# An attention and dense kernel with a hand-written order: third buffer for the input, seven norms on GpSimd, constants first, last stores on two queues, another order

## The chip, the cores and the metric

One Trainium2 chip, one core of it. The metric is device time in microseconds (us) of one execution. Five engines run side by side, each through its own instructions in order: TensorE (PE; its weight loads are PEld), VectorE (DVE), ScalarE (ACT), GpSimd (POOL) and SyncE (SP), which here only issues DMAs. They wait for each other by semaphores.

## What is computed

x is 2048 rows of 512. It is normalised row by row; the result xn feeds two branches, and both are added to x.

```python
x = A_x
xn = _layernorm(x, axis=-1)
return x + _A_ref(xn, A_wq, A_wk, A_wv, A_wo, A_beta) + _B_ref(xn, B_w1, B_w2)
# _B_ref: silu(xn @ w1) @ w2, with 1792 hidden columns
# _A_ref: 32 heads of 16, 4 segments of L = 512 rows; for each segment s:
logits = jnp.einsum('bhqd,bhkd->bhqk', qs, ks) * scale + mask
a_dot = jnp.einsum('bhqk,bhkd->bhqd', _softmax(logits), vs)
num = jnp.einsum('bhld,bhde->bhle', phi(qs), M)
den = jnp.einsum('bhld,bhd->bhl', phi(qs), z)[..., None] + 1e-06
o = g * num / den + (1.0 - g) * a_dot        # then o @ wo over all segments
M, z = M + phi(ks)^T vs, z + sum(phi(ks))    # phi(t): t + 1 above 0, exp(t) below
```

## The kernel before

**Order.** Nothing is scheduled by the framework. The string ORDER (lines 16 to 98) holds words, and the loop at the end of the kernel (from line 795) calls for each word a small function that emits its instructions. So the place of a word in the list is the place of its instructions in the queue of every engine that it uses, its DMAs on SP's included. Each line of the list begins with an S word. There are 80; the stretch from one to the next is called a section here.

**Words.** `S`t (scores, line 653): t counts segment, group dt of 8 heads (four) and batch b (five); four row-tiled matmuls per part write the 4-bank PSUM tile psS, of which there is one; the exponential of 2048 columns on ScalarE (L669) makes Pb, and GpSimd masks its diagonal blocks (L677), one pass or two. `E` and `O` (weigh, L696) multiply Pb with v into a PSUM bank psV for the even and odd heads; `Ev`, `Ov` copy it out on DVE and `Ea`, `Oa` on ScalarE (L719, L726), and each then issues DMAs on SP: two that gather sums into zraw (L711) and, for odd heads, four that move rows into oraw (L730). `k`, `q`, `v`, `h` are the dense products, in parts of half or a quarter; `kv`, `qv`, `vv` copy their banks on DVE, `va`, `qa`, `ka` on ScalarE; `kv` also makes kTo on GpSimd (L362), the masked copy that half of the scores read. `ha`, `hv` are tanh on ScalarE and the rest of silu on DVE (L457, L462). `fp`, `fa`, `fv` make phi(K) on GpSimd, ScalarE and DVE, `gp`, `ga`, `gv` phi(Q) in the tile phiQT; `t`, `m`, `mv`, `mw` the memory M. `s`, `sv`, `r`, `w` and `R`, `W` are the denominators and their reciprocals (R and W for the last segment); `z`, `d` spread them by two DMAs each on SP (L542), `zv`, `dv` multiply by them, `n`, `nv` the memory's product and its addition to oT. `o`, `oc`, `od`, `oh` are parts of the output products over 14 rows of hT (0 to 13) and 4 of oT (14 to 17); `st` and `sh` add x and store.

**Norms.** `xs` (or `xc`, `xd`) takes the statistics of a tile of 128 rows, `xg` the roots for four tiles on GpSimd (L283, L286), `Nv`t the norm on DVE and `Na`t the same on GpSimd (ln_norm, L301). Tiles 0 to 3 are turned by TensorE (`X`), the others by a transposing DMA on SP (`XD`, L749).

**Buffers.** x tiles 0 to 3 lie in x_lo, which takes oT's buffer, 4 to 11 in x_hi, one of two hT buffers, 12 to 15 in x_end, one of two phiQT buffers. PSUM has eight banks: four for psS, four that all other products share, each free again when its copy has run. In the last segment psS becomes the place of the outputs of row tiles 2 and 3 once the last exponential has read it.

**Shapes.** Score matmuls use row tiles of the array, E and O column tiles; the dense products behind an S word are emitted whole (L322) or in four column tiles (L324) so as to fit the next such word.

Of the kernel before, what the change touches and what calls it, by code (L numbers as in the profile page):

```python
# [25 lines left out]
S4 qv1.1 k1.1.1 vv1.3 fv0.3 k1.0.0 k1.0.1 k1.0.2 lw0 h0.4.0 k1.1.2 Ev1 h0.4.1 k1.0.3 k1.1.3 kv1.1
S17 h0.8.0 h0.8.1 kv1.0 h0.4.2 O0 xs10 h0.4.3 h0.2.0 Ov0 ha0.4
S10 h0.2.1 k1.2.0 xs11 xs9 k1.2.1 h0.2.2 k1.2.2 h0.2.3 h0.8.2 ha0.2 t0.3 hv0.4 xg8.4 t0.0 k1.2.3
S8 hv0.2 q1.0.0 q1.0.1 q1.0.2 kv1.2 q1.0.3 h0.8.3 q1.2.0 ha0.8 q1.2.1 q1.2.2 h0.6.0 fp0.1
S13 q1.2.3 h0.6.1 qv1.0 xs15 O1 h0.6.2 qv1.2 Ov1 v1.2.0 Nv11 fa0.1 hv0.8 h0.6.3 Nv9  # L30
S12 h1.11.0 h1.11.1 v1.2.1 fv0.1 h1.11.2 k1.3.0 h1.11.3 k1.3.1 ha0.6 k1.3.2 k1.3.3 Nv10 fp1.1
S11 kv1.3 XD11 v1.2.2 t0.1 v1.2.3 m0.2 ha1.11 hv0.6 q1.3.0 mv0.2 vv1.2 q1.3.1 h0.3.0
S14 fa1.1 h0.0.0 XD9 q1.3.2 q1.3.3 Nv8 h0.3.1 h0.3.2 hv1.11 E2
S15 h0.0.1 h0.0.2 gp1.0 qv1.3 v1.0.0 Ev2 v1.0.1 v1.0.2 xs13 h0.0.3 ha0.0 xg12.4 v1.0.3 fv1.1 h1.9.0 vv1.0 XD8 hv0.0
S16 h1.9.1 h0.3.3 m0.0 h0.9.0 ha0.3 mv0.0 h1.9.2 h1.9.3 ha1.9 XD10 xl0.0 O2
S19 h0.9.1 Ov2 hv1.9 h0.9.2 E3 h0.9.3 h0.12.0 h0.12.1 Nv12 h0.12.2 Ev3 ha0.9
S18 hv0.3 bmask k2.2.0 h1.0.0 h0.12.3 ha0.12 k2.2.1 h1.0.1 h1.0.2 h1.0.3
S22 kv2.2 v2.1.0 hv0.9 hv0.12 kind ha1.0 tanh O3 h1.8.0 v2.1.1 h1.8.1
# [5 lines left out]
S25 h1.5.0 Nv13 h1.5.1 h1.5.2 z0.2 z0.1 o0.0.7 O4 oc0.2.2.1 Ov4 ga1.0 zv0.0 od0.2.0.1
S27 gv1.0 q2.1.0 oc0.2.9.1 o0.0.1 h1.5.3 fv1.2 ha1.5 o0.2.6 q2.1.1 gp1.1 qv2.1 o0.2.17
S29 o0.2.14 o0.2.3 oc0.0.4.1 o0.1.2 zv0.1 zv0.2 fp1.0 o0.1.13 o0.0.14 o0.1.0 ga1.1 hv1.5 oc0.1.12.1 o0.1.6 o0.1.11
S28 o0.2.12 h1.1.0 fa1.0 XD12 h1.1.1 o0.1.14 o0.2.5 o0.0.16 o0.1.16 o0.2.11 mw0.0 h1.1.2
S30 o0.1.9 o0.2.10 mw0.2 od0.2.0.3 h1.1.3 o0.0.17 od0.1.8.1 o0.0.15 o0.2.15 od0.2.0.2 o0.2.8 ha1.1 o0.2.16
S33 fv1.0 st0.0 hv1.1 h1.3.0 od0.2.0.0 h1.3.1 h1.3.2 od0.1.8.3 h1.3.3 Nv15 oc0.1.10.1 XD15 st0.2 XD13 gv1.1 ha1.3 hv1.3 E5 fp1.3 od0.1.8.2 o0.1.4
# [7 lines left out]
S39 od0.3.10.0 oc0.3.11.1 h1.2.0 o0.3.8 o0.3.16 kv3.1 gv1.3 h1.2.1 h1.2.2 oc0.3.11.0 xl1.2 E7 fa2.3
S43 gv1.2 h1.2.3 od0.3.10.2 ha1.2 o0.3.7 qv3.3 o0.3.1 O7 od0.3.10.1 fp2.3 Ev7 Ov7 m1.2 oc0.3.13.1
S45 o0.3.12 q3.0.0 hv1.2 ga2.2 q3.0.1 q3.1.0 q3.1.1
S40 mv1.2 m1.0 o0.3.17 oc0.3.13.0 qv3.0 fp2.1 qv3.1 fv2.3 mv1.0 fa2.1 o0.3.15 s1 o0.3.3 st0.3 sv1 h2.3.0  # L60
S46 r1.2 r1.1 h2.3.1 h2.4.0 v3.3.0 ha2.3 xl1.0 v3.3.1 h1.7.0
S41 r1.0 h2.4.1 ha2.4 vv3.3 v3.0.0 v3.0.1 t2.0 hv2.3 r1.3 w1 h1.7.1 d1.2 h1.7.2 z1.2 h1.7.3
# [11 lines left out]
S57 t2.1 o1.1.2 o1.1.14 st1.0 o1.1.6 h2.1.1 o1.1.8 t2.3 hv2.7 h2.11.0 oc1.1.4.0 ha2.1 od1.1.7.1 od1.1.7.0
S56 h2.11.1 o1.1.5 ha2.11 o1.3.0 o1.3.16 o1.3.15 gp2.1 o1.3.14 o1.3.8 xl1.1 hv2.1 o1.1.10 xl1.3
S59 o1.1.1 o1.1.16 O10 hv2.11 oc1.3.10.1 o1.3.3 o1.3.4 ga2.1 h2.6.0 st1.1
S58 Ov10 gp3.3 E11 oc1.3.1.0 gv2.1 m2.0 o1.3.13 Ev11 h2.6.1 ha2.6 o1.3.11 mv2.0
S62 h2.5.0 O11 h2.5.1 o1.3.5 hv2.6 od1.3.12.0 od1.3.12.3 Ov11 ha2.5 s2 hv2.5 gv3.3
S60 od1.3.12.1 h2.13.0 h2.13.1 od1.3.12.2 o1.3.9 ha2.13 o1.3.2 hv2.13 o1.3.7 o1.3.6 oc1.3.1.1
S64 k3.3.0 gp3.0 o1.3.17 oc1.3.10.0 st1.3 k3.3.1 h2.10.0 h2.10.1 ka3.3 ha2.10 sv2  # L80
S61 o2.3.0 h3.1.0 r2.2 h2.9.0 o2.3.5 h2.9.1 oc2.3.2.1 oc2.3.13.1 h3.1.1 r2.0 r2.1 r2.3 o2.3.3 xl3.2 ha2.9 hv2.10 gp3.2 ha3.1
S63 o2.3.6 o2.3.4 t2.2 o2.3.11 w2 hv3.1 h3.3.0 h3.3.1 hv2.9 ha3.3 m2.2
S67 d2.1 d2.3 mv2.2 fill z2.3 hv3.3 h3.0.0 oc2.3.2.0 E12 h3.0.1 ha3.0 Ev12 h3.4.0
S66 hv3.0 od2.3.9.3 o2.0.3 dv2.1 o2.0.0 h3.4.1 h2.12.0 h2.12.1 ha2.12 o2.0.10 zv2.3 hv2.12
S65 o2.0.4 oc2.3.13.0 o2.0.13 o2.0.11 oc2.0.6.1 dv2.3 o2.0.5 o2.3.8 o2.3.7 n2.3 z2.1 o2.0.1 mw2.2 ha3.4
# [748 lines left out]
```

## Time and profile before

| what | value |
|---|---|
| three runs, median (lowest to highest) | 229.09 us (228.93 to 229.31) |
| the profiled execution, its own time | 229.25 us |
| its span, first to last instruction | 227.4 us |
| granted TensorE clock | 1.000 |
| first scores, 80th scores (L662) | 12.45, 205.48 us |
| exponentials (L669) | 80, mean 1878 ns, 150.2 us together |
| masks (L677) | 112, mean 720 ns |
| norms on DVE (L301): x_lo, x_hi, x_end | 413, 535, 499 ns mean |
| idle of ScalarE before exponentials for want of scores | 4.0 us in 9 waits |

In the profile a line gives start and length in us, engine, line of the kernel, operation, tiles written and read, shapes and count; square brackets hold idle time before it and what ended it. SPq and ACTq are issues of DMAs. A busy TensorE is not one at its peak, since matmuls are pipelined and their ends are modelled; the distance of two starts tells what one takes.

### The profile page before, as it was taken

Reading aid. Unit: us, or ns where it says so; the run is one execution under the profiler, and the core shown is the slowest. Engines: PE = TensorE matmul, PEld = TensorE weight load, DVE = VectorE, ACT = ScalarE, POOL = GpSimd, SP = SyncE. Lnnn points to the kernel's source line nnn. Section 1 sums busy time; section 2 is a strip of 40 time slices with the busy share of each in tenths; the row PEclk is TensorE's granted clock in tenths of the full one; section 3 lists DMA queues with packets and bytes.
Section 4 is the critical chain, followed back from the end, with each engine's and each line's share of the span. In section 5 each row is a group of like instructions: output and inputs, shape, how many; then the busy total and the mean of one; then the engine's idle time right before and its main releaser. Section 6 shows DMA issues by size and latency. Waiting matters only on the chain.

```text
span 227.4 us, 7551 instructions
## 1 busy us (share of the span) xinstructions
PE 217.5 (96%) x3127; PEld 113.3 (50%) x3155; DVE 177.1 (78%) x350; ACT 198.5 (87%) x180; POOL 113.9 (50%) x173
## 2 busy tenths in 40 slices
PE   8999999999999999999999999999999999999993
...
ACT  3799998999999999999999899999999989897000
...
GB/s 189 369 379 46 85 36 313 62 45 66 61 22 156 73 35 48 95 34 100 36 61 87 90 45 59 32 119 40 37 93 65 80 40 81 31 68 128 16 95 95
DMA packets 34787, 20.55 MB, mean 90 GB/s; under 512 B 15680, under 2 KB 34240, under 8 KB 34752
## 3 DMA queue, kind: packets, MB, share of 16 engines
...
q8 instruction: 24, 0.39, 0.7%
...
HBM read 9.96 MB, written 2.10 MB: 53 GB/s over the span
## 4 chain that ended last, share of the span: by engine, by line
PE 67%; ACT 17%; DVE 7%; issue 4%; POOL 2%; DMA 1%; DVEq 0%; SPq 0%; ACTq 0%
PE ps L322 20%; PE psO L322 13%; ACT Pb L669 12%; PE psO L324 8%; PE psS L662 8%; PE ps L324 6%; PE psV L696 5%; PE psS L324 3%; ACT th L457 3%; PE psS L756 2%; ACT ex L395 1%; DVE hT L462 1%; DVE kT L361 1%; DVE qT L371 1%; DVE xn_t L301 1%
## 5 line engine op out<-in xcount | busy, mean ns | idle before, releaser
L669 ACT ACTIVATE Pb<-psS 128x2048 bf16<-128x2048 f32 x80 | 150.2, 1878 | 4.7 <-PE psS L662 4.0
L677 POOL TENSOR_SCALAR_AFFINE_SELECT Pb<-Pb 128x512 bf16<-128x512 bf16 (+1 forms) x112 | 79.1, 720 | 84.3 <-ACT Pb L669 83.0
L462 DVE SCALAR_TENSOR_TENSOR hT<-th,ps 128x512 bf16<-128x512 bf16 x56 | 37.7, 679 | 14.4 <-ACT th L457 13.7
L322 PE MATMUL ps<-xnT,w_sb 128*128 128x512 bf16 (+1 forms) x177 | 43.3, 340 | 0.8 <-issue 0.5
L322 PE MATMUL psO<-w_sb,hT 128*128 128x512 bf16 (+2 forms) x137 | 36.0, 339 | 0.7 <-issue 0.5
L457 ACT ACTIVATE th<-ps 128x512 bf16<-128x512 f32 x56 | 32.8, 598 | 0.6 <-PE ps L322 0.6
L324 PE MATMUL psO<-w_sb,hT 128*32 128x512 bf16 (+2 forms) x476 | 27.6, 301 | 0.0
L322 PEld LDWEIGHTS <-w_sb 128*128 128x128 bf16 x184 | 17.1, 98 | 16.3 <-issue 3.3
L696 PE MATMUL psV<-Pb,Vz 128*32 128x128 bf16 (+3 forms) x512 | 23.1, 300 | 0.2
L324 PE MATMUL ps<-xnT,w_sb 128*32 128x512 bf16 (+1 forms) x384 | 21.8, 329 | 0.0
L322 PEld LDWEIGHTS <-hT 128*128 128x128 bf16 x147 | 13.4, 98 | 16.6 <-issue 4.8
L324 PEld LDWEIGHTS <-hT 128*32 128x32 bf16 x644 | 15.9, 97 | 9.3 <-issue 1.7
L662 PE MATMUL psS<-qT,kT 16*128 16x128 bf16 (+3 forms) x256 | 17.3, 301 | 0.9 <-ACT Pb L669 0.8
L696 PEld LDWEIGHTS <-Vz 128*32 128x32 bf16 x512 | 13.1, 96 | 10.3 <-DVE hT L462 1.1
L662 PE MATMUL psS<-qT,kTo 32*128 32x384 bf16 (+3 forms) x256 | 17.2, 299 | 0.6 <-ACT Pb L669 0.2
L362 POOL TENSOR_SCALAR kTo<-kT,pm_odd 128x512 bf16<-128x512 bf16 x16 | 12.3, 771 | 8.4 <-DVE kT L361 7.5
L322 PE MATMUL ps<-xnT,wk_sb 128*128 128x512 bf16 (+1 forms) x66 | 15.4, 328 | 0.7 <-issue 0.5
L322 PE MATMUL ps<-wv_sb,xnT 128*128 128x512 bf16 x48 | 14.3, 380 | 0.6 <-DVE odd L726 0.2
L662 PEld LDWEIGHTS <-kT 16*128 16x128 bf16 x256 | 5.9, 91 | 16.7 <-issue 16.2
L361 DVE CAST kT<-ps 128x512 bf16<-128x512 f32 x15 | 10.2, 689 | 4.9 <-PE ps L322 4.3
L322 PE MATMUL ps<-xnT,wq_sb 128*128 128x256 bf16 (+1 forms) x62 | 12.8, 324 | 0.4 <-issue 0.2
L726 DVE CAST odd<-psV 128x512 bf16<-128x512 f32 x15 | 10.3, 687 | 3.5 <-PE psV L696 3.4
...
## 6 DMA issues: line engine op xcount, KB each, us to landing
...
oraw<-odd SPq DMA_DIRECT2D x64, 16.0 KB
...
```

Of the source, the lines that this page charges most:

```text
L322: return [nc.tensor.matmul(out, lhsT=lhsT, rhs=rhs, start=start, stop=stop, skip_group_check=True)]
L324: nc.tensor.matmul(out[c : c + 32], lhsT=lhsT[:, c : c + 32], rhs=rhs, start=start, stop=stop, tile_position=(0, c), skip_group_check=True,)
L361: copy(out=kT[:, dt, :], in_=sts[s].pop(("k", dt))[:, :])
L362: nc.gpsimd.tensor_scalar(out=kTo[:, dt, :], in0=kT[:, dt, :], scalar1=pm_odd[:, 0:1], scalar2=1.0, op0=ALU.mult, op1=ALU.mult,)
L457: nc.scalar.activation(out=th[:], in_=sts[s]["h", ft][:, :], func=AF.Tanh, scale=0.5)
L462: nc.vector.scalar_tensor_tensor(out=st["hT"][:, ft, :], in0=st.pop(("th", ft))[:], scalar=1.0, in1=st.pop(("h", ft))[:, :], op0=ALU.add, ...
L662: nc.tensor.matmul(psS[:, g, c0 : c0 + nq], lhsT=kk[rows, dt, kt * P : (kt + 1) * P], rhs=st["qT"][rows, dt, kt * P : L], start=True, stop ...
L669: exp = nc.scalar.activation(out=Pb[:, :, :], in_=psS[:, :, :], func=AF.Exp, scale=SCALE)
L677: mask = nc.gpsimd.affine_select(out=blocks, in_=blocks, compare_op=ALU.is_ge, fill=0.0, base=0, pattern=[[0, blocks.shape[1]], [1, P]], c ...
L696: nc.tensor.matmul(psV[32 * g : 32 * g + 32, kt * P : L], lhsT=Vzs[s % 2][:, kt, 4 * dt + g, par : par + 2, :].rearrange("p a d -> p (a d) ...
L726: copy(out=odd[:], in_=sts[s].pop(("psV", 1))[:, :])
L756: nc.tensor.matmul(idle[:, 0:P], lhsT=zraw[:, 0:P], rhs=zraw[:, 0:P], start=True, stop=True)
```

## The change

A third home for x: tiles 8 to 11 go to x_mid, the first use of the tag phiQT, and x_end is the second. x_hi now holds tiles 4 to 7 alone. Norms 4, 6, 8, 9, 10, 12 and 14 are `Na` words. `kind` and `odd` (DVE) stand at the head of the list. v0.3 is copied by ScalarE (`va0.3`) and q0.1 by DVE (`qv0.1`). The stores of the last segment's even row tiles and of the first half of its last one go to ScalarE's queue. And the whole list has another order; the number of matmul columns is the same.

```diff
+    x_mid = segp.tile([P, TPS, D], BF16, name="x_mid", tag="phiQT")
     x_end = segp.tile([P, TPS, D], BF16, name="x_end", tag="phiQT")
 
     def xs(t0, t1):
         if t0 >= NT - TPS:
             return x_end[:, t0 - NT + TPS : t1 - NT + TPS, :]
+        if t0 >= 2 * TPS:
+            return x_mid[:, t0 - 2 * TPS : t1 - 2 * TPS, :]
         return x_lo[:, t0:t1, :] if t1 <= TPS else x_hi[:, t0 - TPS : t1 - TPS, :]
...
     def store(s, j):
...
-        nc.sync.dma_start(out=out_flat[t * P : (t + 1) * P, :], in_=o_out[:])
+        queue = nc.scalar if s == LAST and j % 2 == 0 else nc.sync
+        queue.dma_start(out=out_flat[t * P : (t + 1) * P, :], in_=o_out[:])
...
     def half_store(h):
...
-        nc.sync.dma_start(out=out_flat[(NT - 1) * P : NT * P, cols], in_=o_half[:])
+        queue = nc.sync if h else nc.scalar
+        queue.dma_start(out=out_flat[(NT - 1) * P : NT * P, cols], in_=o_half[:])
```

The list, its head and its end (the middle is left out):

```diff
 ORDER = """
-ones0 ones1 zeros xc0 xd0 xc1 xq0 xi0 Nv0 busy44 xd1 xq1 xc2 xi1 X0.1 Nv1 xd2 Xa0.1 busy6 v0.0.0 v0.0.1 xq2 X1.1 Xa1.1 xs3 v0.0.2 v0.0.3 xq3 v0.1.0 xi2 v0.1.1 v0.1.2 v0.1.3 odd Nv2 xi3 X2.1 va0.0 k0.2.0 va0.1 Nv3 Xv2.1 X3.1 Xv3.1 k0.0.0 k0.0.1 k0.0.2 k0.0.3 q0.0.0 kv0.0 tb q0.0.1 q0.0.2 xs4 q0.0.3 qa0.0 k0.2.1 q0.3.0 fa0.0 q0.1.0
-S1 k0.2.2 xs6 q0.1.1 v0.3.0 v0.3.1 xs7 q0.3.1 q0.1.2 q0.1.3 xs5 xg4.4 q0.3.2 qa0.1 q0.3.3 fp0.0
-S2 k0.2.3 v0.3.2 qv0.3 v0.3.3 k0.1.0 kv0.2 fp0.2 fa0.2 k0.1.1 vv0.3 k0.1.2 k0.1.3 q0.2.0 q0.2.1
-S3 kv0.1 q0.2.2 h0.10.0 h0.10.1 Nv4 fv0.0 q0.2.3 h0.10.2 v0.2.0 h0.10.3 qv0.2 ha0.10 k0.3.0 k0.3.1
-S0 Nv5 v0.2.1 k0.3.2 hv0.10 h0.11.0 k0.3.3 h0.11.1 h0.11.2 kv0.3 h0.11.3 Nv7 xs8 XD5 ha0.11 h0.7.0
-S7 h0.7.1 h0.1.0 h0.7.2 h0.7.3 v0.2.2 h0.1.1 v0.2.3 XD4 h0.1.2 h0.1.3 hv0.11 Nv6 ha0.7
-S6 h0.13.0 fp0.3 XD7 h0.13.1 vv0.2 hv0.7 E0 XD6 v1.1.0 h0.13.2 h0.13.3 ha0.1 v1.1.1 Ev0
-S5 fv0.2 h0.5.0 v1.1.2 h0.5.1 hv0.1 v1.1.3 vv1.1 v1.3.0 h0.5.2 ha0.13 xs14 hv0.13 h0.5.3 ha0.5 t0.2 v1.3.1
...
-S74 o2.3.16 h3.12.0 st2.3 h3.12.1 ha3.12 h3.2.0 gv3.1 E14
-S73 h3.2.1 ha3.2 Ev14 oc2.2.5.1 o2.1.2 o2.2.16 o2.1.6 hv3.12 h3.8.0 o2.2.10 st2.2 hv3.2 o2.1.1 o2.1.5 h3.8.1 ha3.8 hv3.8
-S79 o2.1.0 O14 Ov14 od2.1.12.2 s3 sv3 r3.1 o2.1.7 r3.3 h3.7.0 r3.2 r3.0 oc2.1.10.0 od2.1.12.3 o2.1.3 w3
-S77 h3.6.0 R0.0 oc2.1.11.0 h3.7.1 R0.1 ha3.7 h3.6.1 hv3.7 d3.2 o2.1.14 R0.3 h3.9.0 ha3.6 hv3.6 o2.1.15
-S76 o2.1.8 d3.0 d3.1 h3.9.1 o2.1.9 oc2.1.10.1 h3.13.0 ha3.9 od2.1.12.0 oc2.1.11.1 h3.13.1 xl3.3 hv3.9 o3.0.12 o2.1.16 ha3.13 o2.1.13
-S75 o3.0.5 hv3.13 o2.1.4 o3.0.4 R0.2 W0 o2.1.17 z3.0 h3.10.0 o3.1.8 h3.10.1 dv3.0 z3.2 ha3.10 od2.1.12.1 st2.1 o3.0.0 o3.1.6
-S78 o3.0.9 hv3.10 dv3.1 o3.1.1 h3.11.0 o3.0.8 h3.11.1 dv3.2 E15 oh13.1 oh4.1 ha3.11 z3.1 o3.2.13 Ea15 oh12.1 hv3.11 oh6.1 oh10.1 o3.2.1 O15 Oa15 oh11.1 oh2.1 oh12.0 o3.0.1 zv3.0 oh13.0 n3.1 od3.1.11.3 oh3.1 zv3.1 o3.2.0 oh10.0 n3.0 o3.1.2 nv3.0 o3.0.7 nv3.1 o3.1.12 oh9.1 oh8.0 o3.2.5 oh11.0 o3.1.7 o3.2.6 o3.0.13 oh8.1 R1.1 R1.0 o3.2.9 o3.1.14 d3.3 R1.3 o3.2.14 oc3.0.3.0 oh0.0 o3.0.6 o3.2.8 oc3.0.11.1 zv3.2 o3.1.10 n3.2 o3.2.10 oh9.0 R1.2 oh1.1 oh15.0 W1 nv3.2 oh15.1 o3.2.4 oc3.0.11.0 o3.1.5 o3.0.14 o3.2.11 oh1.0 o3.2.12 o3.2.2 oh6.0 o3.2.16 oh2.0 z3.3 oh7.0 oh0.1 dv3.3 oh3.0 od3.0.10.0 oh14.0 od3.1.11.1 oc3.1.0.0 o3.0.15 zv3.3 od3.1.11.0 oc3.0.3.1 n3.3 oc3.1.9.0 oh4.0 o3.2.3 xl3.0 o3.1.16 nv3.3 o3.2.15 od3.0.10.1 od3.0.10.2 o3.2.7 oh5.0 oh16.0 oh16.1 od3.0.10.3 oh14.1 o3.2.17 oh17.0 oh17.1 o3.0.2 o3.0.16 o3.0.17 od3.1.11.2 xl3.1 st3.2 oc3.1.9.1 oh7.1 oh5.1 sh0 o3.1.17 sh1 oc3.1.0.1 o3.1.3 o3.1.15 o3.1.13 st3.0 o3.1.4 st3.1
+kind odd ones0 ones1 zeros xc0 xd0 xc1 xq0 xi0 Nv0 busy44 xd1 xq1 xc2 xi1 X0.1 Nv1 xd2 Xa0.1 busy6 v0.0.0 v0.0.1 xq2 X1.1 Xa1.1 xs3 v0.0.2 v0.0.3 xq3 v0.1.0 v0.1.1 va0.0 xi2 Nv2 v0.1.2 v0.1.3 tb X2.1 xi3 Nv3 k0.2.0 X3.1 k0.2.1 Xv2.1 k0.0.0 k0.0.1 Xv3.1 k0.0.2 k0.0.3 q0.0.0 va0.1 kv0.0 q0.0.1 q0.0.2 q0.0.3 k0.2.2 k0.2.3 qa0.0 v0.3.0 fa0.0
+S0 xs4 q0.3.0 q0.3.1 k0.1.0 v0.3.1 v0.3.2 v0.3.3 kv0.2 va0.3 xs6 xs5 fp0.2 q0.3.2 q0.1.0 k0.1.1
+S2 q0.3.3 k0.3.0 qv0.3 k0.1.2 xs7 q0.1.1 k0.3.1 q0.1.2 xg4.4 q0.1.3 fa0.2 qv0.1 Na4 k0.3.2 k0.1.3
+S1 h0.1.0 kv0.1 k0.3.3 h0.10.0 h0.10.1 q0.2.0 h0.1.1 h0.10.2 kv0.3 h0.10.3 ha0.10
+S5 h0.7.0 fv0.2 Nv5 h0.7.1 tanh t0.2 h0.7.2 Na6 q0.2.1 h0.7.3 h0.1.2 q0.2.2 h0.1.3 ha0.7 hv0.10 q0.2.3 xs8 xs10
+S6 v0.2.0 v0.2.1 qv0.2 v0.2.2 Nv7 h0.11.0 h0.11.1 h0.11.2 v0.2.3 h0.11.3 hv0.7 vv0.2 ha0.1 XD5
+S3 v1.1.0 h0.5.0 v1.1.1 h0.5.1 XD4 hv0.1 h0.5.2 XD7 v1.1.2 ha0.11 v1.1.3 h0.5.3 vv1.1 h0.13.0 ha0.5 XD6 fp0.1 hv0.5
+S7 h0.13.1 xs9 h0.13.2 E0 h0.13.3 ha0.13 v1.3.0 hv0.11 v1.3.1
+S4 Ev0 v1.3.2 fp0.3 v1.3.3 hv0.13 E1 k1.2.0 xs11 k1.2.1 fa0.3 q1.1.0 Ev1 q1.1.1 xg8.4 vv1.3
...
+S25 h1.3.0 o0.2.14 gv1.0 h1.3.1 h1.3.2 h1.1.2 o0.2.15 h1.1.3 oc0.1.12.1 o0.2.16 ha1.1 Nv13 XD13 od0.2.0.1 od0.1.8.0 fp1.2
...
+S60 h2.9.0 h3.1.0 h3.1.1 hv2.10 o2.3.5 h2.9.1 h3.3.0 xl2.3 o2.3.1 ha3.1 r2.0 w2 hv3.1 d2.1 ha2.9 hv2.9
...
+S73 oc2.1.10.1 h3.2.1 xl3.2 hv3.12 o2.1.3 xl3.1 hv3.5 h3.8.0 xl3.3 gv3.0 E14 oc2.1.10.0 ha3.2 Ev14 hv3.2 h3.8.1 ha3.8 hv3.8
+S77 od2.1.12.3 o2.1.2 O14 h3.6.0 Ov14 s3 sv3 h3.6.1 o2.1.13 ha3.6
+S78 r3.0 od2.1.12.1 r3.1 h3.13.0 h3.9.0 oc2.1.11.0 r3.2 h3.9.1 ha3.9 hv3.6 r3.3 h3.13.1 o2.1.5 w3 ha3.13
+S76 d3.2 h3.10.0 od2.1.12.0 hv3.13 o2.1.16 R0.0 h3.10.1 R0.1 ha3.10 hv3.9 hv3.10 o2.1.1 o2.1.9 R0.3 o2.1.15 o3.0.4 R0.2 W0 o3.0.5 dv3.2
+S75 d3.1 o2.1.14 h3.7.0 h3.7.1 h3.11.0 o2.1.4 d3.0 ha3.7 o3.0.0 o3.0.6 hv3.7 o3.0.9 h3.11.1 o3.0.13 ha3.11
+S79 o2.1.8 o3.1.7 oc3.0.3.1 o2.1.17 hv3.11 o3.1.1 o3.0.8 z3.2 E15 oc3.0.11.0 od2.1.12.2 o3.1.8 dv3.1 zv3.2 z3.0 oh4.1 od3.1.11.2 z3.1 o3.1.6 o3.2.3 oh1.0 oc3.1.9.0 o3.1.5 st2.1 dv3.0 zv3.1 O15 Ea15 od3.0.10.3 od3.1.11.0 zv3.0 oh3.0 o3.2.5 oh9.0 o3.1.12 n3.1 o3.2.12 Oa15 oh5.1 oh11.1 oc3.0.3.0 oh11.0 o3.2.11 oh2.0 n3.0 o3.2.9 od3.0.10.0 nv3.1 oc3.0.11.1 o3.2.6 nv3.0 oh6.1 oh15.0 R1.0 o3.0.7 R1.1 oh14.1 o3.2.10 oh13.0 oh12.1 R1.2 n3.2 oh15.1 oh13.1 o3.2.13 o3.2.2 oh3.1 R1.3 oc3.1.0.0 oh10.0 oh5.0 oh7.0 oh4.0 o3.1.2 o3.2.14 o3.0.1 W1 o3.2.1 od3.0.10.1 o3.2.4 o3.0.14 nv3.2 oh9.1 o3.2.7 o3.2.8 o3.1.16 o3.2.16 oh16.1 o3.0.15 d3.3 dv3.3 o3.0.16 oc3.1.9.1 z3.3 zv3.3 oh0.1 o3.2.0 o3.0.2 oh7.1 xl3.0 n3.3 od3.1.11.3 od3.1.11.1 o3.1.14 od3.0.10.2 o3.2.15 o3.0.12 oh8.0 oh0.0 o3.1.13 nv3.3 oh14.0 o3.2.17 oh10.1 oh17.1 o3.0.17 oh6.0 oh2.1 oh16.0 o3.1.10 st3.2 oh12.0 oh1.1 o3.1.15 oh17.0 o3.1.4 st3.0 sh0 oh8.1 o3.1.3 o3.1.17 oc3.1.0.1 sh1 st3.1
 """
```

More of the change, by code (lines that the diff above doesn't have):

```diff
@@ L26 @@
[L26 to L38, printed above, removed]
@@ L44 @@
[L44 to L49, printed above, removed]
@@ L57 @@
[L57 to L62, printed above, removed]
@@ L74 @@
[L74 to L85, printed above, removed]
```

93 lines of the change are left out of this document (64 added, 29 removed).

## The prediction

> **What bounds the kernel now.** I read the page's engine table and its slices first, then the timeline of ScalarE and TensorE in the middle, then the table of waits, then the queue of SP at the end.
>
> ```profile
> PE 217.5 (96%) x3127; PEld 113.3 (50%) x3155; DVE 177.1 (78%) x350; ACT 198.5 (87%) x180; POOL 113.9 (50%) x173
> PE   8999999999999999999999999999999999999993
> ACT  3799998999999999999999899999999989897000
> ```
>
> Two engines look full: TensorE over the whole span, ScalarE from the third slice to the 37th. Which of them sets the pace is seen in the timeline of each.
>
> ```profile
> 106.85 1.88 ACT L669 ACTIVATE Pb<-psS 128x2048 bf16<-128x2048 f32 x1
> 108.62 0.62 ACT L395 ACTIVATE ex<-kT 128x512 bf16<-128x512 bf16 x1
> 109.22 1.88 ACT L669 ACTIVATE Pb<-psS 128x2048 bf16<-128x2048 f32 x1
> ...
> 108.77 0.40 PE L662 MATMUL psS<-qT,kTo 32*128 32x512 bf16 x4
> 109.10 0.40 PE L324 MATMUL ps<-xnT,w_sb 128*32 128x512 bf16 x4
> ```
>
> An exponential ends at 108.73, the next scores start at 108.77 into the same PSUM tile, and the next exponential starts 0.45 us later, at 109.22. That is a ring of two engines: 1.88 + 0.04 + 0.45 = 2.37 to 2.38 us per score word, whatever else is on either engine. One filler of ScalarE (0.59 to 0.65) fits into the 0.45 us, since its tail overlaps; with two it does not fit:
>
> ```profile
> 27.51 1.88 ACT L669 ACTIVATE Pb<-psS 128x2048 bf16<-128x2048 f32 x1
> 29.29 1.08 ACT L457 ACTIVATE th<-ps 128x512 bf16<-128x512 f32 x2
> 30.24 1.90 ACT L669 ACTIVATE Pb<-psS 128x2048 bf16<-128x2048 f32 x1
> ```
>
> Here the step is 2.73, so a second filler costs 0.355. TensorE's own need in a section (from one S word to the next) is its columns, 0.215 per 512 (109.10 to 109.33 above, within reading), plus 0.21 for the two changes between score matmuls and the others (68.03 to 68.34 and 68.34 to 68.67 in its timeline, each less 0.215). A section of ten 512-column units so needs 2.36: TensorE is filled to just under the ring. The span has three parts: first scores at 12.45, the ring up to the 80th scores at 205.48 (193.03), and 21.93 behind them.
>
> In the ring, 79 steps of 2.38 are 188.0; seven sections with two fillers add 2.5; twelve sections whose columns need more than the ring allows add 2.2 (0.47, 0.39, 0.33 and 0.28 the largest, all from the 64th section on); one wait adds 0.29. The sum is 193.0, which the trace has. The wait is this one:
>
> ```profile
> 22.40 0.10 PEld L662 LDWEIGHTS <-kTo 32*128 32x128 bf16 x4 [0.28 <-POOL kTo L362]
> ```
>
> Behind the last scores a chain through SP sets the end:
>
> ```profile
> 210.48 1.05 SPq L711 DMA_DIRECT2D zraw<-odd  x2
> 211.64 3.54 SPq L730 DMA_DIRECT2D oraw<-odd  x4
> 215.23 2.73 SPq L542 DMA_DIRECT2D spr<-rz  x4
> ...
> 219.50 0.43 DVE L554 TENSOR_TENSOR oT<-spr,oraw 128x512 bf16<-128x512 bf16 x1 [0.87 <-DMA spr<-rz]
> ...
> 224.18 0.81 SPq L591 DMA_DIRECT2D out_dram<-o_out  x2
> ```
>
> O15 runs at 209.07, its copy ends at 210.43, and SP then issues ten DMAs without a pause (the two of d3.3 and the two of z3.3 last). The last pair of spreads lands for zv3.3 at 219.50, n_add ends at 220.72, and the products of the last oT row start at 220.78: 11.71 after O15. TensorE ends at 223.62; the last store's DVE work ends at 224.43, SP issues it at 224.62, and the span ends at 227.41.
>
> **The change, part by part.** Matmul columns are the same in number (counted over both programs), and so are the 79 pairs of shape changes.
>
> *Constants first.* kind and odd are six small DVE instructions, 0.21+0.15+0.14+0.16+0.15+0.14 = 0.95. They now stand before the first statistics, where DVE waits 2.51 for x (it is idle from 1.05 to 3.56). Their inputs are done on GpSimd at 1.35 and 1.92. Nothing is paid; if x came at once, up to 0.95 would be.
>
> *Start.* Ahead of q0.0, whose copy opens the first scores, the list now holds one part of k0.2 more, two matmuls of 256 columns, 0.22. Against that the v0.1 copy and its bank no longer stand before k0.0 (which in the trace starts at 9.79, 0.17 after it could). From 0 to +0.22; I take +0.1.
>
> *x tiles 8 to 11.* Same load, same place on SP. The buffer is wanted again by gv1.0, twelve sections (28 us) after the last norm that reads it, and x_hi is free earlier. Nothing.
>
> *Seven norms to GpSimd.* DVE loses 7 x about 0.5 (L301: 535 and 499 mean). GpSimd, 50% busy, gains 7 x 0.69, taking the kTo row (0.69 median, one pointer scalar) as nearest; the bounds are 0.41 (DVE's own) and 1.14 (its longest pass over a tile). GpSimd's order puts each behind a mask that waits for its exponential, and the next mask comes 2.38 later, so 0.64 + 0.69 fits. Neither engine is in the ring: nothing, unless a mask or a copy comes late (rivals).
>
> *ACT and DVE copies.* va0.3 goes to ScalarE and qa0.1 leaves it: 0.59 against 0.58.
>
> *The list in the ring.* I counted the words that put work on ScalarE between S words: nine sections now have two full fillers instead of seven, +2 x 0.355 = +0.71. By columns, ten sections need more than their ring step instead of twelve, 1.80 instead of 2.21: -0.41 (the largest are now S75 with 0.71 and S60 with 0.28). The kTo wait goes: kv0.1 stood one section before the scores that read it and now stands four before, -0.29. Together 0.0. What new waits there are I can't see in the trace of before; from below 0 (no further wait is left to remove), from above about 1.0 (three waits of the kTo kind). I take 0, since the closest pairs of copy and next user of the bank are not closer than before: fewer than 0.8 us of columns apart in 5 places against 9.
>
> *Tail.* O15 comes 3.44 after the last scores by columns (3.12, the scores' 0.215, one change) where it came 3.59 after, held by hv3.11's bank; that word now ends earlier: -0.15. The chain of 11.71 keeps its ten issues in the same order: 0. Behind it stand 2.58 of columns instead of 2.64: -0.06.
>
> *Stores on two queues.* The last SP issue waited for the one before (224.18 to 224.52, then 224.62) though its data was there at 224.43. With every other store on ScalarE's queue, idle since 210.43, SP is free and starts 0.03 after the data: -0.16. An issue on ScalarE costs no work there; its bounds are 0 and 0.45, which lies beside DVE's last 0.69.
>
> Sum: +0.1 + 0.0 - 0.15 - 0.06 - 0.16 = -0.27. The profiled execution took 229.25 with a span of 227.4 (1.85 outside it), so 228.98; that execution lies 0.16 above the median of the runs, 229.09, which makes 228.8.
>
> **The rivals.**
>
> *The chain behind O15 gets shorter (faster).* The fourth oraw<-odd issue takes most of the 3.54: 1.68 where the others take 0.57. A fetch of instructions, 16 KB on another queue, lay at 213.33 to 214.80 in the trace (the page counts 24 such transfers), and most oraw issues elsewhere take 0.57. If the new order meets no fetch there, the chain loses 1.1; TensorE then bounds it, since its columns up to the first product of the last row need 14.37 after the last scores against 15.15 by the chain, so -0.78: 228.0. Against it: fetches follow each other every 4 to 6 us at this end, so a hit is likelier than not.
>
> *SP runs late before O15 (slower).* W0 now comes after three d moves, and z3.2, z3.0, z3.1, a store and the two moves of E15's sums follow it on SP: six issues of 0.63, 0.46 and 2 x 0.57, 5.4 us. By the DVE rows (reciprocals 0.5, hT 0.68) W0 ends some 0.9 before the 80th scores, so SP is through about 4.6 after them; the copy of O15 is ready 4.8 after. In the trace of before SP was through at 210.38 and the copy at 210.43, so so small a margin is not new. Each us that W0, z3.2 or st2.1 is later than 0.2 goes to the end in full; from 0.9 late the result is slower than 0.2%: with 1 us, +0.8 - 0.27, 229.6.
>
> *GpSimd's norms hold up DVE (slower).* The trace has this kind of collision:
>
> ```profile
> 18.00 1.14 POOL L677 TENSOR_SCALAR_AFFINE_SELECT Pb<-Pb 128x1024 bf16<-128x1024 bf16 x1
> 18.11 1.57 DVE L405 SCALAR_TENSOR_TENSOR pk<-ex,pos 128x512 bf16<-128x512 bf16 x1
> ```
>
> pk takes 0.69 elsewhere and here 1.57, beside a GpSimd pass; casts from PSUM keep 0.69 throughout. If a pushed DVE operation has a copy behind it that frees a bank, TensorE is late and the ring moves by what exceeds its slack (0.02). Two of the seven, at up to 0.69 each, give +1.4 - 0.27: 230.2; one gives 229.5. For it: banks are tight. Against: the masks do this 96 times now, and no wait of the ring comes from it. [...]
>
> **How the numbers follow.** Forecast (228.8, nothing new in the ring, a shorter end): 0.42. Chain shorter, 228.0: 0.24. SP late, 229.6: 0.16. DVE held up or another new wait in the ring, 229.5 to 230.2: 0.18. The runs lie within 0.2%, 0.46 us, so less than that is no change. Faster, below 228.63: the second case and a third of the first, 0.38. Slower, above 229.55: three fifths of the third and two thirds of the fourth, 0.22. Same: 0.40. The range for 8 in 10 reaches from a shorter chain with no extra start, 227.8, to one late norm and a late SP queue, 230.0; the forecast's own is 228.4 to 229.2.
>
> **What would show it.** Right: first scores at 12.5 to 12.7; steps of 2.38, nine of 2.73; 80th scores near 205.6; O15 3.4 behind, the last row 11.7 behind that; last issue on SP at once after its data. Wrong: a PE wait on DVE or GpSimd in the ring, 80th scores after 206.3, or a pause in SP's issues between W0 and the sums of O15.

## The result and the profile after

The changed kernel takes 230.97 us, the median of four runs (230.42 to 231.27); the kernel before took 229.19 beside it. The ratio is 1.0077, with a 95% interval of 1.0055 to 1.0098: slower by 0.8%, where 0.1% faster had been forecast. The profiled execution took 230.91, its span 228.9.

| stretch of the profiled execution, us | before | forecast, change | after |
|---|---|---|---|
| span's start to first scores | 12.45 | +0.1 | 12.53 |
| first to 80th scores | 193.03 | 0.0 | 193.55 |
| 80th scores to the span's end | 21.9 | -0.37 | 22.8 |
| outside the span | 1.85 | 0 | 2.0 |

Half a microsecond is lost in the ring, nearly one behind it, and 0.2 outside the span. The page's engine table and GpSimd's slices (40 equal parts of the span, tenths busy) come first:

```profile
PE 220.2 (96%) x3173; PEld 113.8 (50%) x3173; DVE 173.5 (76%) x343; ACT 198.2 (87%) x180; POOL 127.5 (56%) x180
POOL 6049977998898746656634763545633554332000
```

GpSimd has gained seven instructions and 13.6 us, far more than seven times 0.69. The list of the line that holds the norms says why (engine, operation, tiles, count, then shortest, median and longest in ns, first and last start):

```profile
L304 POOL TENSOR_SCALAR xn_t<-x_mid,mv_all,rstd_all x3: 2062/2062/2066, 43.3 to 49.4; 128x512 bf16<-128x512 bf16 x3
L304 DVE TENSOR_SCALAR xn_t<-x_hi,mv_all,rstd_all x2: 411/424/437, 19.8 to 23.0; 128x512 bf16<-128x512 bf16 x2
```

A norm takes 2.06 on GpSimd, where kTo, of the same shape, takes 0.69; kTo has one scalar per row, the norm two, and no run shows whether that makes the difference. VectorE needs 0.41.

TensorE's waits, the whole span (us in total, times, the longest one):

```profile
PE ps L327 <- DVE phiQT L567: 1.7, 1, 1.7
PE psS L761 <- DVE zraw L194: 1.1, 1, 1.1
PE psS L667 <- ACT Pb L674: 0.8, 2, 0.4
PE psV L701 <- DVE hT L465: 0.5, 1, 0.5
PE psV L701 <- POOL Pb L682: 0.2, 1, 0.2
```

The first is new and is in the tail; the second is the start, the third the ring itself, and the last two are new and in sections 18 to 20 (a section is numbered here by the exponential that ends it: the 18th is the step from the 17th exponential to the 18th). The tail's wait, in the timeline of SP, VectorE and TensorE (answers to the prediction's last fence):

```profile
212.10 3.37 SPq L735 DMA_DIRECT2D oraw<-odd  x4
215.52 3.76 SPq L545 DMA_DIRECT2D spr<-rz  x4
...
220.38 0.42 DVE L567 TENSOR_TENSOR phiQT<-spr,phiQT 128x512 bf16<-128x512 bf16 x1 [4.26 <-DMA spr<-rz]
...
220.85 0.40 PE L327 MATMUL ps<-phiQT,Mbf 128*32 128x512 bf16 x4 [1.69 <-DVE phiQT L567]
```

And the chain that ended last says how long the spread itself took:

```profile
216.23 4.05 DMA spr<-rz
```

Other spreads take about 2.0 in the same chain (205.65 and 208.35: 1.98 and 1.99). This one was issued on time, 0.03 behind its predecessor, and took twice as long to land. VectorE stood 4.26, TensorE 1.69 (n3.3 wants dv3.3's result).

What held it is in the view of the DMA queues, cut to 217.5 to 219.0:

```profile
DMA  2394454544410000000025445464543000010101
...
q1 hardware_dynamic: 241, 0.12, 26.7%
q8 instruction: 1, 0.02, 5.2%
```

Queue 8 moves one packet of 16 KB: 5.2% of 16 engines over 1.5 us is 1.25 us (its record has 1.24, from 217.61 on). The page counts 25 such packets and 6,346 TensorE instructions, one for some 254 of them. They are taken here for its fetches of instructions; e4 bears that out, where 128 instructions more bring them earlier. A fetch that holds a DMA is called a hit below. In the packet records the two spreads issued at 216.23 and 217.01 move 112 of their 128 packets of 512 bytes at once, and the 16 left of the first follow one by one from 218.85 on, when that fetch is done. The fourth spread's issue on SP, 0.60 as a rule, takes 1.62 from 217.66 on; an oraw issue takes 1.50 from 212.72 on, 0.03 behind the start of the fetch before.

### The profile page after: what moved, and what is told of

It reads as the page before. It is cut to its first block, busy times and chain, and to the rows that moved or that the text cites. A ratio compares the mean times of both kernels' runs of the same rounds, so it can differ in the third digit from the quotient of the medians.

```text
span 228.9 us, 7620 instructions
## 1 busy us (share of the span) xinstructions
PE 220.2 (96%) x3173; PEld 113.8 (50%) x3173; DVE 173.5 (76%) x343; ACT 198.2 (87%) x180; POOL 127.5 (56%) x180
## 4 chain that ended last, share of the span: by engine, by line
PE 71%; ACT 9%; POOL 6%; DVE 5%; DMA 4%; SPq 2%; issue 2%; DVEq 0%; POOLq 0%; ACTq 0%
PE ps L325 20%; PE psO L325 13%; PE psS L667 10%; PE ps L327 9%; PE psO L327 8%; PE psV L701 7%; ACT Pb L674 6%; DMA spr<-rz 4%; POOL xn_t L304 2%; PE psS L761 2%; POOL Pb L682 2%; ACT th L460 2%; SPq L735 1%; POOL kTo L365 1%; DVE hT L465 1%
## 5 line engine op out<-in xcount | busy, mean ns | idle before, releaser
L325 PE MATMUL ps<-xnT,w_sb 128*128 128x512 bf16 (+1 forms) x198 | 47.7, 341 | 0.0
L465 DVE SCALAR_TENSOR_TENSOR hT<-th,ps 128x512 bf16<-128x512 bf16 x56 | 37.7, 680 | 12.8 <-ACT th L460 12.3
L327 PE MATMUL psO<-w_sb,hT 128*32 128x512 bf16 (+2 forms) x520 | 30.5, 310 | 0.0
L325 PEld LDWEIGHTS <-w_sb 128*128 128x128 bf16 x198 | 18.3, 98 | 17.3 <-issue 4.3
L327 PEld LDWEIGHTS <-hT 128*32 128x32 bf16 x688 | 16.7, 97 | 10.1 <-issue 2.9
L325 PEld LDWEIGHTS <-hT 128*128 128x128 bf16 x136 | 12.5, 98 | 14.9 <-issue 3.2
L327 PE MATMUL ps<-xnT,w_sb 128*32 128x512 bf16 (+1 forms) x328 | 18.9, 328 | 0.0
L667 PE MATMUL psS<-qT,kT 16*128 16x256 bf16 (+3 forms) x256 | 17.3, 301 | 0.9 <-ACT Pb L674 0.3
L325 PE MATMUL ps<-wv_sb,xnT 128*128 128x512 bf16 x53 | 15.3, 380 | 0.0
L325 PE MATMUL ps<-xnT,wq_sb 128*128 128x512 bf16 (+1 forms) x68 | 15.2, 329 | 0.0
L724 DVE CAST oraw<-psV 128x512 bf16<-128x512 f32 x15 | 10.2, 683 | 4.2 <-PE psV L701 4.1
```

What stands on the lines that cost most here:

```text
L325: return [nc.tensor.matmul(out, lhsT=lhsT, rhs=rhs, start=start, stop=stop, skip_group_check=True)]
L327: nc.tensor.matmul(out[c : c + 32], lhsT=lhsT[:, c : c + 32], rhs=rhs, start=start, stop=stop, tile_position=(0, c), skip_group_check=True,)
L465: nc.vector.scalar_tensor_tensor(out=st["hT"][:, ft, :], in0=st.pop(("th", ft))[:], scalar=1.0, in1=st.pop(("h", ft))[:, :], op0=ALU.add, ...
L667: nc.tensor.matmul(psS[:, g, c0 : c0 + nq], lhsT=kk[rows, dt, kt * P : (kt + 1) * P], rhs=st["qT"][rows, dt, kt * P : L], start=True, stop ...
L724: copy(out=oraw[:], in_=sts[s].pop(("psV", 0))[:, :])
```

## The experiments

The time of the kernel before, measured beside each batch, was 229.22 (e1 to e4), 228.94 (e5 to e8), 229.12 (e9 to e12) and 228.98 (e13, e14).

**e1: the norms back on VectorE.** In the list, for each of 4, 6, 8, 9, 10, 12 and 14:

```diff
-Na4
+Nv4
```

> The changed kernel with its seven Na words made Nv again, in the same places; all else stays. Theory A (a norm on GpSimd takes 2.06 us, so masks come late and TensorE and the copies behind it wait in sections 18 to 20): the excess of those three sections over 2.38, now 0.47 + 0.14 + 0.39 = 1.00, falls to 0.35 + 0.10 or less, the 80th scores start at 205.4 to 205.6 instead of 206.08, and as TensorE's instructions stay the same the tail keeps its 22.8, so the time is 230.3 to 230.5. Rival (the three late sections come from the order of the list, not from the norms): 80th scores at 206.0 to 206.3, time 230.8 to 231.2, or more, since VectorE has seven norms of about 0.5 more.

Measured: 236.34 (1.0297, 1.0248 to 1.0347), 5.4 slower than the change, and the 80th scores at 213.58. Both theories fall. The norm of tile 4 stands right behind the roots in the list, and they end on GpSimd at 19.8; on VectorE it holds up what stands behind it there, the two kT copies, and TensorE waits for their bank:

```profile
19.84 0.72 DVE L304 TENSOR_SCALAR xn_t<-x_hi,mv_all,rstd_all 128x512 bf16<-128x512 bf16 x1 [2.07 <-POOL rstd_all L289]
20.48 1.27 DVE L364 CAST kT<-ps 128x512 bf16<-128x512 f32 x2
...
21.21 0.58 PE L325 MATMUL ps<-xnT,wq_sb 128*128 128x256 bf16 x2 [2.51 <-DVE kT L364]
```

In this wait the granted clock falls, which makes it dearer: from 20.4 to 27.2 it is 0.50, and six matmuls of 256 columns take 1.48 there (21.59) where six take 0.82 behind it (28.40). In slices of 5.9 us:

```profile
PEclk9997699999999999999999999999999999999999
```

Later waits of TensorE for VectorE, 1.3 and 1.2, add to the loss. So this list needs its norms on GpSimd, however dear they are there.

**e2: the products behind O15 whole.** Behind the call of each word's function:

```diff
+        if word == "O15":
+            now = "whole"
```

> The changed kernel with all products behind O15 emitted whole (one matmul and one weight load) and not in four column tiles (four and four): the same columns, about a quarter of TensorE's instructions there. Theory F (a 16 KB fetch of TensorE's instructions, one for every 256 of them, occupies one of the 16 DMA engines for 1 to 1.3 us; the one at 217.5 to 218.85 held the issue and the packets of the last spreads, the one at 212.5 to 213.8 an oraw issue): at most one fetch is left between 209 and 222, the spread d3.3 lands about 2.0 after its issue instead of 4.05, TensorE's wait of 1.69 goes, the tail from the 80th scores to the end falls from 22.8 to 20.6 to 21.3, the time is 228.8 to 229.5. Rival (the order of the list sets the wait: dv3.3 and n3.3 stand too early on DVE and TensorE, and the spreads land when they land): the spread keeps about 4 us, the tail stays within 0.3 of 22.8, the time within 0.4 of 231.0.

Measured: 228.99 (0.9994, 0.9968 to 1.0019), 2.0 faster than the change. The tail is 20.9, TensorE waits nowhere in it, and SP's issues show no pause:

```profile
211.85 2.45 SPq L735 DMA_DIRECT2D oraw<-odd  x4
214.35 2.73 SPq L545 DMA_DIRECT2D spr<-rz  x4
```

Beside the changed kernel's lines the eight issues last 5.23 instead of 7.18. The last addition to oT ends 10.66 behind O15 instead of 12.89. Theory F holds.

**e3: e1 and e2 together.**

> The two edits of e1 and e2 together. Theories A and F: the two add up, 80th scores at 205.4 to 205.6 and a tail of 20.6 to 21.3, time 228.2 to 229.0. If only F holds 228.8 to 229.5, if only A 230.3 to 230.5, if neither 230.8 to 231.2.

Measured: 234.21 (1.0216, 1.0179 to 1.0252), none of the four cases. The 2.1 to e1 are not the tail's: that is 21.5 in e1 and 21.2 here, and the ring has 201.05 and 199.04, at a granted clock of 0.985 and 0.993 over the span. e1 has the change's TensorE instructions, and its last fetch ahead of the last row comes 8.16 behind O15 where the change's comes 8.05; yet it starts behind SP's last issue, not ahead of it, and holds nothing. So the second hit hangs on a few tenths of a microsecond. That it came in all four runs of the change is likely by their spans (228.4 to 229.2), but only the profiled one shows it.

**e4: the same fetches, half a period earlier.** In the helper that emits a product, 64 times from S30 on, for whole products of 512 columns that do not open their bank:

```diff
+            return [
+                nc.tensor.matmul(
+                    out[:, c : c + HL], lhsT=lhsT, rhs=rhs[:, c : c + HL], start=start, stop=stop, skip_group_check=True
+                )
+                for c in (0, HL)
+            ]
```

> The changed kernel with 64 whole matmuls of 512 columns in the middle of the ring (from the 31st section on) split into two of 256: the same columns, 128 TensorE instructions more (64 weight loads, 64 matmuls), so each later fetch of instructions comes half a period earlier. Theory F: the fetches of the tail move from 212.7 and 217.6 to about 210.5 and 215.2, each holds SP's issues for about 1.0, but none lies on the packets of the last spreads; d3.3 lands about 2 after its issue, the tail falls by 0.6 to 1.5, the time is 229.5 to 230.5. Rival (order of the list): tail and time unchanged within 0.3; if the splits cost something in the ring, the time is longer.

Measured: 229.56 (1.0021, 0.9998 to 1.0044), 1.4 faster than the change with 128 instructions more. The fetches of the tail lie at 211.1 and 215.3, no issue is held, the last addition ends 10.79 behind O15, and the tail is 20.8. That the fetches would hold SP for 1.0 each was wrong: at these places they hold nothing. The ring is 0.6 longer, but not by the splits: 0.46 of it is one event, a transposing DMA of phi(K) that SP issues 0.18 behind the start of a fetch (165.36). Here it is, and then the same DMA in e2:

```profile
165.54 2.13 SPq L426 DMA_TRANSPOSE phiK<-pk  x1
```

```profile
165.76 1.22 SPq L416 DMA_TRANSPOSE phiK<-pk  x1
```

Moving the fetches moves their price: out of the tail, and a part of it to this place.

**e5: one of the two norms in a row off GpSimd** (on e2).

```diff
-... fa0.1 Na8 h0.6.2 Na10 gate ...
+... fa0.1 Na8 h0.6.2 gate ...
...
-... XD8 E2 qv1.3 h1.9.3 ...
+... XD8 E2 qv1.3 Nv10 XD10 h1.9.3 ...
```

> The kernel of e2 (changed kernel, tail emitted whole) with one norm, that of tile 10, moved from GpSimd to VectorE: it leaves the pair of norms in which GpSimd stood for 4.12 us and runs one word behind qv1.3 two sections later, where VectorE idled 1.19; its transposing DMA goes behind it. Theory A2 (the fall of e1 was VectorE waiting for roots and moved copies, not a proof that the pair on GpSimd is free; six masks stood behind it, and E2 waited for one): GpSimd's queue has the masks of S10 and S12 2 us earlier, E2's wait of 0.15 goes, the excess over 2.38 of sections 18 to 20 falls from 1.00 to 0.35 to 0.7, and the time from first to 80th scores from 193.68 to 193.0 to 193.4; the time to 228.3 to 228.8. Rival (the list's copies and tanhs set these three sections whatever GpSimd does): 193.6 to 193.8 and 228.9 to 229.1.

Measured: 229.06 (1.0015, 1.0000 to 1.0030), e2's time. The pair and the masks behind it stand like this in the changed kernel:

```profile
47.30 4.12 POOL L304 TENSOR_SCALAR xn_t<-x_mid,mv_all,rstd_all 128x512 bf16<-128x512 bf16 x2
...
51.38 4.02 POOL L682 TENSOR_SCALAR_AFFINE_SELECT Pb<-Pb 128x512 bf16<-128x512 bf16 x6
...
53.10 0.29 PE L701 MATMUL psV<-Pb,Vz 128*32 128x256 bf16 x4 [0.15 <-POOL Pb L682]
```

With one norm less, E2's wait goes and the 18th section falls from 2.85 to 2.73, but sections 19 and 20 keep 2.56 and 2.76. Of the ring's 0.5 this pair of norms accounts for 0.1 to 0.2 (0.12 in section 18; the ring is 193.50 against 193.68); the rest stays, as the rival had it.

**e6: all stores on SP** (on e2).

```diff
-        queue = nc.scalar if s == LAST and j % 2 == 0 else nc.sync
+        queue = nc.sync
...
-        queue = nc.sync if h else nc.scalar
+        queue = nc.sync
```

> The kernel of e2 with the last segment's stores all on SP's queue again. By the prediction's step the last issue waits for the one before it and the time grows by 0.16 against e2, 229.15. By the changed kernel's profile the stores' data come 0.35 and more apart, so SP is free each time: 0.0 within 0.1, 228.9 to 229.1. Rival (a second queue adds to what lies outside the span, which was 1.85 before and 2.0 to 2.1 after and in e2): the time falls by 0.1 to 0.3.

Measured: 229.38 (1.0031, 1.0013 to 1.0049). The last issue starts 0.17 behind its data (VectorE ends at 224.62, SP issues at 224.79); in e2 it is 0.03, in the change 0.02. From TensorE's end to the span's end it takes 3.71 instead of 3.53. The prediction's 0.16 was right, and what I had read off the changed profile before this run was not. In the profiled execution a fetch also held a store's issue by 0.8, ahead of O15's sums, and the tail is 0.7 longer than e2's in all. The time outside the span stays at 2.06, so the second queue does not make it.

**e7: the kernel before with its tail whole.** The edit is e2's.

> The kernel before with the products behind O15 emitted whole. Theory F: its chain behind O15, 11.65 to the end of the last addition, holds one fetch on an oraw issue (1.68 where the others take 0.57) and falls to 10.6 to 10.8, as in e2 and e4 (10.66, 10.79); then TensorE's columns bound the tail, which goes from 21.9 to 21.0 to 21.4: 228.3 to 228.7. Rival (fetches matter only in the changed kernel): 229.0 to 229.4.

Measured: 229.06 (1.0003, 0.9990 to 1.0016). The chain gets shorter as expected, from 11.65 to 10.78, and the time does not. In the kernel before, TensorE's products and the chain through SP were nearly even. The view of its tail by stretches (length, TensorE busy, instructions, granted clock, DMA share, GB/s) shows TensorE busy up to the last row of oT:

```profile
215.00:218.00 3.00, 3.00 (x88) 1.00 0.18 51
218.00:220.80 2.80, 2.79 (x92) 1.00 0.51 138
```

But the ends of matmuls are modelled, and a short wait is seen only in their starts. The last addition to oT ends at 220.72, and around it stand these products:

```profile
220.47 0.30 PE L324 MATMUL psS<-wo_sb,oT 128*32 128x256 bf16 x4
220.78 0.40 PE L324 MATMUL psS<-wo_sb,oT 128*32 128x512 bf16 x4
```

The start of a product of 256 columns is followed by the next one 0.11 later (220.20 and 220.31 just before); here it is 0.31. So TensorE did wait for the chain, but for 0.20 only. With the chain 0.87 shorter, TensorE ends 17.98 behind the last scores instead of 18.13: the products bound the rest. After the change the stretch 218 to 221 reads:

```profile
218.00:221.00 3.00, 1.31 (x32) 1.00 0.34 90
```

**e8: the kernel before with the seven norms on GpSimd.** Nv4 and the six others become Na4 and so on, in their places.

> The kernel before with the same seven norms on GpSimd in their old places, nothing else. At 2.06 each: GpSimd, which in the trace of before has no pause from 16.15 to 23.76, gets two of them there, kTo for the fifth section's scores comes 2 to 4 later and TensorE waits for it, and the scores behind; later pairs cost little: the time from first to 80th scores goes from 193.0 to 195 to 198, the time to 231 to 234. Rival (as the prediction had it: GpSimd is half idle and a norm there costs 0.7): within 0.5 of 229.2.

Measured: 241.17 (1.0557, 1.0524 to 1.0590), far above the range expected. The largest loss is not where I looked for it. The norms of tiles 8 to 11 read x_hi, which is a buffer of hT; late on GpSimd, they hold the first silu that writes hT there:

```profile
58.44 0.69 DVE L462 SCALAR_TENSOR_TENSOR hT<-th,ps 128x512 bf16<-128x512 bf16 x1 [7.24 <-POOL xn_t L301]
```

**e9: constants out of the head** (on e2). `odd` goes back before the third norm. `kind` goes before `gate`, into S15's line; in the list before, kind and gate stood in the lines of S22 and S23, so its old place is not what this run tries.

```diff
-kind odd ones0 ...
+ones0 ...
...
-... xi2 Nv2 ...
+... xi2 odd Nv2 ...
...
-... Na10 gate ...
+... Na10 kind gate ...
```

> The kernel of e2 with odd put back before the third norm and kind before gate. Theory: the constants cost and bring nothing in the ring or the tail (within 0.2). One thing is open: all kernels made from the changed one take 2.0 to 2.1 outside their span, those from the kernel before 1.7 to 1.85. If the constants at the head make that difference, the time outside falls to 1.8 and the time to 228.7; if not, it stays at 2.0 to 2.1 and the time at 229.0.

Measured: 229.99 (1.0033, 1.0015 to 1.0051), 1.0 above e2. In the middle of the ring the five instructions of kind (0.81 together) push the odd copy behind them, and the 15th section takes 0.77 more; the ring as a whole takes 0.6 more (194.27 against 193.68). The start of this execution came 0.38 later, which executions do by themselves (first scores between 12.0 and 12.8 in all of them). Outside the span it is 2.2, no less than in e2.

**e10: tiles 8 to 11 back in x_hi** (on e2). The two edits of the diff that name x_mid are undone.

> The kernel of e2 with tiles 8 to 11 of x back in x_hi, the first hT buffer. Theory (as the prediction has it: the buffers are wanted long after the norms): ring, tail and time as in e2, 229.0 within 0.2. If the third home makes the 0.25 more outside the span, that falls to 1.8; if x_hi comes free later and holds up the second segment's h words, a wait of TensorE on VectorE appears near S16 and the time grows by its length.

Measured: 229.87 (1.0025, 1.0006 to 1.0045). The wait that was named as the other case is there, 0.77 in the 18th section, and another 0.8 in the tail is a fetch that held a spread's issue by 1.3:

```profile
51.06 0.69 DVE L462 SCALAR_TENSOR_TENSOR hT<-th,ps 128x512 bf16<-128x512 bf16 x1 [2.15 <-POOL xn_t L301]
```

So the third home, which the prediction costed at nothing, is what the norms on GpSimd need: 0.7 of ring (194.38 against 193.68). Whether the fetch in the tail comes of it is not shown.

**e11: e5 and e9 on e2.**

> The edits of e5 and e9 on e2: tail emitted whole, norm of tile 10 on VectorE, constants back in their places. The best that the runs so far point to: 0.1 to 0.2 from e5 in the ring and, if e9 brings its 0.25, 228.6 to 228.8; else 228.9 to 229.1, which is the kernel before.

Measured: 230.16 (1.0041, 1.0023 to 1.0060), with e9's 0.76 in the 15th section and a fetch on a spread's issue at 208.9.

**e12: the kernel before with e4's splits.**

> The kernel before with the 64 splits of e4 (128 TensorE instructions more from the 31st section on), so that the fetch at 219.2 of its tail comes at about 216.4, on the packets of the last spreads, and the one at 213.3 at about 210.5. The splits themselves cost about 0.6 in the ring (194.18 against 193.55 in e4). Theory F2 (a fetch on the last spreads delays them by 1 to 2 and shows in the time only by what TensorE then lacks of ready products): the last multiply for oT comes 0.5 to 2 later after O15 than the 10.86 of before, TensorE idles up to 1.5 near the last row, and the tail grows from 21.9 to 22.2 to 23.4. Rival (only the changed kernel's order is sensitive): tail within 0.2 of 21.9, TensorE without a gap.

Measured: 229.35 (1.0010, 0.9985 to 1.0035). The fetch does come at 216.24, between the last spreads, and delays none of their packets; the tail is 21.8, the last multiply 10.77 behind O15. The theory's place was met and its effect stayed out: this fetch lay on a transfer and did not hold it. An earlier fetch, at 205.04, did hold: a spread's issue at 205.27 takes 1.60 instead of 0.60, SP comes to O15's sums 1.0 late (211.50, the copy ends at 210.46), and the last addition ends 11.57 behind O15 although no issue behind O15 is held.

**e13: the copy of z out of GpSimd's way** (on e2).

```diff
-S19 fp1.1 h0.12.0 mv0.0 h0.9.3 h1.0.0 hv0.0 E3 ...
+S19 fp1.1 h0.12.0 h0.9.3 h1.0.0 hv0.0 mv0.0 E3 ...
```

> The kernel of e2 with one word moved: mv0.0, the two copies of the memory on VectorE, behind hv0.0 instead of two words ahead of it. Theory C (z's copy, 0.16 alone, takes 0.65 beside a GpSimd mask, pushes hv0.0, and E3 waits 0.52 for its bank): E3's wait falls to 0.1 or less, the excess over 2.38 of section 20 from 0.39 to 0.0 to 0.1, 80th scores 193.3 to 193.4 after the first instead of 193.68, time 228.6 to 228.8. Rival (another copy or the tanh ahead of hv0.0 sets E3's start): E3's wait within 0.15 of 0.52, 193.6 to 193.8, 228.9 to 229.1.

Measured: 229.13 (1.0019, 0.9999 to 1.0038). In the changed kernel a copy of two columns stands beside a mask of 1.09 that starts at 56.44, and E3 waits behind the silu that follows it:

```profile
56.90 0.65 DVE L435 COPY z<-zs 128x2 f32<-128x2 f32 x1
57.46 0.67 DVE L465 SCALAR_TENSOR_TENSOR hT<-th,ps 128x512 bf16<-128x512 bf16 x1
...
58.19 0.73 PE L701 MATMUL psV<-Pb,Vz 128*32 128x512 bf16 x16 [0.52 <-DVE hT L465]
```

In e13 it runs when the mask is over:

```profile
57.69 0.16 DVE L435 COPY z<-zs 128x2 f32<-128x2 f32 x1
```

E3's wait is gone and the 20th section falls from 2.77 to 2.49. But the 21st rises from 2.51 to 2.67, and the ring is 193.65 where it was 193.68. The cause of that wait is shown; what its removal brings is lost again one section later.

**e14: e5 and e13 on e2.**

> The edits of e5 and e13 on e2. If theory C holds, 193.0 to 193.3 from first to 80th scores and 228.4 to 228.7, below both kernels by 0.2 to 0.3% and 1.0%; if not, 193.4 to 193.6 and 228.8 to 229.1.

Measured: 228.98 (1.0005, 0.9989 to 1.0022). Sections 18 to 20 have 0.38 less than in e2, the 21st 0.51 more, in which TensorE waits 0.5 for the bank of another silu. No version beat the kernel before; e2 and e14 equal it and lie 0.9% below the change.

## Why the prediction was wrong, point by point

**The step that failed: "The chain of 11.71 keeps its ten issues in the same order: 0".** The order is the same, but the term is not 0. Two fetches lie on the ten issues, the last addition ends 12.89 behind O15 instead of 11.65, and TensorE runs out of products and stands 1.69. One fetch lay there before too (the oraw issue of 1.68); the second, on the last spreads, is new. Without these hits the chain is 10.66 and 10.79, the tail 20.9 and 20.8, and the time 2.0 and 1.4 below the change (e2, e4). So the two fetches took 2.0 (e2); the one that the kernel before had cost it 0.15 (e7).

**The path.** "Behind the last scores a chain through SP sets the end" is right for the kernel before by 0.20 and no more: that long TensorE waits for the last row of oT, and with the chain 0.87 shorter it ends 0.15 earlier (e7). The prediction did not say how near the next bound stood. After the change the chain bounds by far more, 1.69.

**Luck in the sum.** e2, the change without its hits, has 0.9994 of the time before, with an interval that holds 1, and 0.9988 was forecast. That is not the forecast coming true: in its profile the tail is 1.0 shorter than before (-0.37 was said), the ring 0.65 longer (0.0) and the time outside the span 0.2 longer (0).

**The fetch as a rival.** The first rival, a chain without a fetch, was written down for the better side only, and it describes the tail of e2 and e4: 21.93 - 0.15 - 0.06 - 0.16 - 0.78 makes 20.8, and they have 20.9 and 20.8. Its 228.0 did not come, since ring and the time outside grew. A second hit, on a spread's packets, was not written down.

**Ring.** The forecast's parts are there: the 5th section has lost its wait for kTo (2.41), nine sections have two fillers, the one before S79 takes 3.46 (2.73 and 0.71 were said). What had been taken at 0 of "0 to 1.0" is 0.5. Sections 18 to 20 hold 0.65 beyond their fillers: 0.12 by a mask behind two norms (e5), 0.28 by the copy of z (e13), the rest not traced; 0.13 is gained elsewhere. Taking either cause away shortened the ring by only 0.18 and 0.03, so what holds the 0.5 is not shown. The wait that e13 removes is of the third rival's kind, a VectorE operation that takes longer beside a GpSimd pass, with a silu behind it whose bank TensorE wants; it was a mask that it stood beside, not a norm: z's copy took 0.65 beside it (56.90) and 0.16 behind it (e13). The norms themselves held up little: of 29 VectorE operations that ran beside them in the changed kernel one was longer than its kind, a pk at 65.42 with 1.04 instead of 0.69, and z's other copy took 0.16 beside a norm (48.35).

**Norms on GpSimd: mis-sized by three.** 2.06 instead of 0.69, outside the bounds of 0.41 and 1.14; the trace of before shows no long operation with two scalars per row on that engine, and the bounds should have been wider for it. One norm less on GpSimd did not change the time (e5); what the seven cost together is not shown, since on VectorE, in these places, they cost more (e1).

**The cheap edits.** The prediction costed the third home and the constants at nothing, by the room that the old order leaves them. In the new order they save ring: the third home 0.7 (e10), the constants at the head 0.6 against the places tried in e9, the norms on GpSimd 7.5 (e1). They belong together, and together with the new order come out at a loss of half a microsecond in the ring.

**Right.** Start +0.08 (+0.1 was said), O15 3.48 behind the last scores (3.44), SP not late ahead of O15's sums (0.03 behind the copy), last issue 0.02 behind its data (e6: 0.16 to 0.18).

**Open.** In the profiled executions all kernels with the new list take 2.0 to 2.2 outside their span, those with the old one 1.7 to 1.85. Neither the second queue (e6), the constants (e9) nor the third home (e10) makes it; what in the list does was not found. And the 0.5 in sections 18 to 21 moves from one silu or copy to the next (e5, e13, e14); which order of copies would free it was not tried.
